# Query features of six tiles turned by VectorE and stored in blocks, and the last gate of pairs one pair sooner

## The chip, the cores and the metric

The kernel runs on one core of a Trainium2 chip. The metric is the device time of one execution in microseconds (us). Before the change the median of three runs is 624.48 us, from 624.06 to 625.14.

The engines are TensorE (PE in the profile; the loading of its weights is PEld), VectorE (DVE), ScalarE (ACT), GpSimd (POOL) and SyncE (SP). Transfers are issued from the queues of SP, ScalarE and GpSimd, each of which works in order, and move on the same 16 DMA engines.

## The reference

The input `x` has 2048 rows of 512. After a layer norm of each row, two branches are computed and added to `x`:

```python
# A: linear attention with 32 heads of 16
q, k, v = split(xn @ wqkv)
phi_q = concat(softmax(q w_phi), softmax(-q w_phi))    # per head: 32 features
phi_k = concat(softmax(k w_phi), softmax(-k w_phi))
kv  = sum_s phi_k v ;  z = sum_s phi_k
o   = (phi_q kv) / (phi_q z + 1e-6)
A   = o @ wo
# B: gated mlp that mixes over the sequence
z   = gelu(xn @ w_in) ;  z1, z2 = halves of z, 688 columns each
g   = w_sp @ layernorm(z2) + b_sp
B   = (z1 * g) @ w_out
out = x + A + B
```

## The kernel before

The 2048 rows are 16 tiles of 128 (`NT = 16`), and the tiles go in 8 pairs (`NP`). Most products are made in three parts of rounded values: a matrix is split into a rounded part and the rest of it, and `mm3` (lines 54 to 58) issues three matmuls. The rounding (L48) and the rest (L52) are helpers, so many operations carry these two lines and are told apart by their tiles.

The work comes in stages. In the first, all 16 tiles are projected; the unnormalised features of the queries, `e`, with the reciprocals of their softmax sums, go to `e_d` in DRAM. In the second and third, `z2` is made and multiplied by `w_sp` in a form with seven products (tile `g`, from about 228 to 488 us). As each pair of row tiles of that product is drained, `gate` (L783) multiplies it by `z1`, turns the result in blocks of 32x32 on VectorE (L796), and stores it with four DMAs, one for each 32 partitions (L799), in `u_d`. The DMAs put every block in its place, so `u_d` holds the whole transpose and can be loaded as it is for the product with `w_out`. The gate of the last pair, tiles 14 and 15, is put off into the last stage, where it is emitted after pair `GATE_LAST`.

The last stage runs from about 488 us to the end. It takes the pairs in order, and for the pair of tiles i and i+1 does the following:
- `project_u(i)` (L960) multiplies the gated rows `u` of tile i by `w_out` into a PSUM tile `pout`, 17 matmuls.
- `attend` (L943) multiplies the turned query features `f` of the pair by `kvT`, 16 products into `po` (32 instructions in the profile). The result is split into a rounded part by ScalarE and a rest by VectorE, tile `oT`.
- `project_u(i+1)` does the same for the other tile.
- `project_o` (L969) multiplies `oT` by `wo` into the same `pout`. ScalarE copies it to `xr` (L984), one of three buffers, and GpSimd's queue adds it to the output with an accumulating DMA (L985). The last tile goes another way, through VectorE and SP.
- `ahead` (L1008), after each tile, emits what later tiles need: `features(i+3)`, the load of `e` for tile i+5 (`et`), the load of `u` for tile i+4.
- `attend_T` (L926) makes the turned features of the next pair: 16 transposes on TensorE into `ptq` (L935 or L937), and four copies by ScalarE into the tiles `f` (L939), of which there are `NG + 1 = 5`, four to a pair.

`features` (L898) calls `q_fin` (L539): VectorE multiplies `e` by the sum of the key features `zb` into a temporary tile (L543, `qtmp`), sums it (L544), makes the reciprocals (L545 to L548) and multiplies `e` by them (L550). Then a DMA on GpSimd's queue copies the features to a tile `er` that TensorE can transpose in its faster type (L906).

The order of the instructions on each engine comes from a planner, which goes through the program in a simulated time and puts on each engine's queue what is ready. `tc.issue_after(x)` holds the instructions emitted inside it behind x, on x's own engine alone; it makes no engine wait for another. So the transposes of a pair stand behind the last product of the pair before on TensorE, and the features of each tile stand behind those of the tile before on VectorE. Semaphores are set by the data and the buffers.

Of the kernel before, what the change touches and what calls it, by code (L numbers as in the profile page):

```python
# [10 lines left out]
F32 = mybir.dt.float32  # L11
# [7 lines left out]
P = 128  # L19
# [4 lines left out]
NG = 4  # L24
NF = 2 * D
# [3 lines left out]
BL = 32  # L29
EPS_LN = 1e-5  # L30
EPS_DEN = 1e-6
XB = 5
FT, LT = 6, 13
NP = NT // 2
HP, QP = P // 2, P // 4
FP = 3 * P
# [4 lines left out]
def mixer(ctx: ExitStack, tc: tile.TileContext, x, x_t, wv, wqkT, phi_bd, wo, w_in, wst, b_r, w_out, out):  # L41
    nc = tc.nc
    pe, act, dve, pool, sp = nc.tensor, nc.scalar, nc.vector, nc.gpsimd, nc.sync
# [27 lines left out]
    def xz_tile(n, dt, name):  # L71
        return xz.tile([P, SL], dt, tag="xz", name=name)[:, :n]

    mid = ctx.enter_context(ExitStack())
    dram = ctx.enter_context(tc.tile_pool(name="dram", bufs=1, space=DRAM))
# [2 lines left out]
    u_d = dram.tile([NT, FU, P], F32, name="u_d")  # L78
    kvT_d = dram.tile([P, D], F32, name="kvT_d")
    zb_d = dram.tile([P, NF], F32, name="zb_d")  # L80
    nm_d = dram.tile([NT, ND, P], F32, name="nm_d")

    ident = cst.tile([P, P], F32, name="ident")
# [13 lines left out]
    def heads(ap):  # L97
        return ap.rearrange("p (h d) -> p h d", d=DH)

    def group(e, j):  # L100

        return e[:, j * P:(j + 1) * P]

    def pairs(ap, a):
        return ap.rearrange("p (h a) -> p h a", a=2)[:, :, a]

    def bc(ap, n):
        return ap.unsqueeze(2).to_broadcast([P, n, DH])
# [25 lines left out]
    def zproj(ps, s, w, order=(0, 1)):  # L134

        if ps in (za, kv_ps_p):
            p = [ps.tile([P, D], F32, tag="z", name="zps") for _ in range(2)]
        else:
            q = ps.tile([P, 2, D], F32, tag="z", name="zps")
            p = [q[:, k] for k in range(2)]  # L140
        t = xT[s]
        for k, j in enumerate(order):
            for c in range(ND):
                cs = slice(c * P, (c + 1) * P)
                zproj.last = mm3(p[k][:, :FC], (t[:, 0, cs], t[:, 1, cs]), (w[j][0][:, c], w[j][1][:, c]), c == 0, c == ND - 1)
        return [(slice(k, k + 1), p[k][:, :FC].unsqueeze(1)) for k in range(2)] if ps in (za, kv_ps_p) else [(slice(0, 2), q[:, :, :FC])]
# [28 lines left out]
    with ExitStack() as p0:  # L175
        res = p0.enter_context(left("p0res", 1))
        wk = p0.enter_context(left("p0wk", 2))
# [234 lines left out]
        t = xz_tile(2 * D, F32R, "xT").rearrange("p (a b) -> p a b", a=2)  # L412
# [18 lines left out]
        p = ps.tile([P, D], F32, tag="mm", name="proj")  # L431
# [7 lines left out]
        p = ps.tile([P, D], F32, tag="mm", name="proj")  # L439
# [18 lines left out]
        p = ps.tile([P, D], F32, tag="mm", name="proj")  # L458
# [80 lines left out]
    def q_fin(et, tmp, zb):  # L539

        e, r, t, w = et[:, :NF], *(et[:, NF + k * 2 * H:NF + (k + 1) * 2 * H] for k in range(3))
        den = et[:, NF + 6 * H:QW]
        dve.tensor_tensor(tmp, e, zb, op=ALU.mult)  # L543
        dve.tensor_reduce(t, heads(tmp), axis=AX.X, op=ALU.add)  # L544
        dve.tensor_tensor(t, t, r, op=ALU.mult)  # L545
        dve.scalar_tensor_tensor(den, pairs(t, 0), EPS_DEN, pairs(t, 1), op0=ALU.add, op1=ALU.add)
        dve.reciprocal(den, den)
        dve.tensor_tensor(w.rearrange("p (h a) -> p h a", a=2), r.rearrange("p (h a) -> p h a", a=2),  # L548
                          den.unsqueeze(2).to_broadcast([P, H, 2]), op=ALU.mult)
        return e, dve.tensor_tensor(heads(e), heads(e), bc(w, 2 * H), op=ALU.mult).ins  # L550

    QC = 4
    NQ = NT // QC
    NC = NP * NQ


    SEQ = [(i, q) for i in range(NP) for q in (range(NQ) if i < NP - 1 else (1, 2, 3, 0))]

# [5 lines left out]
    def load_a(n):  # L564
        i, q = SEQ[n]
        f = []
        for k in range(2):
            t = ws.tile([P, QC, P], F32, tag=f"f{k}", bufs=2, name="wf")
            sp.dma_start(t, wst[2 * i + k, :, q * QC:(q + 1) * QC, :])
            f.append(t.rearrange("p (k two) t -> p two k t", two=2))  # L570
        return f

    def prep_a(n, f):

        a, b = f
        pl = hl[n % 2]
        ops = {}

        def parts(names, src):
            t = pl.tile([P, 2, len(names), 2, P], F32R, tag="".join(names), name="A")  # L580
            prep_a.last = b_parts(t[:, 0], t[:, 1], src)
            for k, m in enumerate(names):
                ops[m] = t[:, 0, k], t[:, 1, k]

        sums = (sm[0].tile([P, 4, 2, P], F32, name="S") if sm else
                zw.tile([P, 4, FC], F32, tag=("T", "z2")[n], bufs=n + 1, name="S").rearrange("p a b -> p (a b)")[:, :8 * P].rearrange("p (a k b) -> p a k b", a=4, k=2))
        parts(("A11", "A12"), a)
        dve.tensor_tensor(sums[:, 0], b[:, 0], b[:, 1], op=ALU.add)
        dve.tensor_tensor(sums[:, 1], sums[:, 0], a[:, 0], op=ALU.subtract)  # L589
        parts(("S1", "S2"), sums[:, 0:2])  # L590
        dve.tensor_tensor(sums[:, 2], a[:, 0], b[:, 0], op=ALU.subtract)
        dve.tensor_tensor(sums[:, 3], a[:, 1], sums[:, 1], op=ALU.subtract)
        parts(("S3", "S4"), sums[:, 2:4])
        parts(("A22",), b[:, 1:2])
        return ops
# [3 lines left out]
    with ExitStack() as p1:  # L599
        tmp1 = p1.enter_context(left("tmp1", 1))  # L600
        kvT = tmp1.tile([P, D], F32, name="kvT")
        zb = tmp1.tile([P, NF], F32, name="zb")
# [41 lines left out]
        for s in range(NE):  # L644
            et = load_q(s, tb.tile([P, QW], F32, name="et") if s else tmp1.tile([P, 4, D], F32, tag="zhl", name="et").rearrange("p a b -> p (a b)")[:, :QW])
            tmp = zw.tile([P, 4, FC], F32, tag="z2", bufs=2, name="qtmp").rearrange("p a b -> p (a b)")[:, :NF]
            e, _ = q_fin(et, tmp, zb)
# [57 lines left out]
    for s in range(NT):  # L705
        p = zproj((kv_ps_p, zc, zbp, za)[s % 4], s, w2, (0, 1) if s % 2 == 0 else (1, 0))
# [7 lines left out]
        for k, q in p:  # L714
            ins = act.activation(z[:, k], q, AF.Gelu_apprx_tanh, scale=r_x[:, s:s + 1]).ins
# [35 lines left out]
    def load_z1(i):  # L751
        t = gt.tile([P, 2, FH + REM], F32, tag="z1", name="z1t")
        for k in range(2):
            pool.dma_start(t[:, k, :FH], z1_d[2 * i + k])  # L754
        return t

    def products(n, g):
        i, q = SEQ[n]
        ops = A.pop(n)
        for name, an, bn in FORM:  # L760
            if n % NQ == 0:
                g[name] = psg.tile([P, D], F32, tag="g", name="g")
            dst = g[name][:, :FC]
            for k in range(2):
                (ah, al), (bh, bl) = ops[an], B[2 * q + k][bn]
                mm3(dst, (ah[:, k], al[:, k]), (bh, bl), n % NQ == 0 and k == 0, n % NQ == NQ - 1 and k == 1)
# [16 lines left out]
    def gate(i, cb, z, u, ut, after=None):  # L783
# [10 lines left out]
        def turn():  # L794
# [3 lines left out]
            for b in range(0, P, BL):  # L798
                (pool if i == NP - 2 else sp).dma_start(dst[:, :, b:b + BL], src[b:b + BL].rearrange("p (m b) -> p m b", b=BL))  # L799

        return turn

    def slot(name, dt=F32):
        return xz_tile(2 * FH, dt, name)
# [44 lines left out]
    g, es, ets = {}, {}, {}  # L849
    for n in range(NC):  # L850
        i = SEQ[n][0]
        if n % NQ == 1 and i < NP - 1:
            z = load_z1(i)
        products(n, g)
        if n % NQ == NQ - 1 and i < NP - 1:
            c = gt.tile([P, 2, FU], F32, tag="c", name="c")
            cq = c[:, :, :FH].rearrange("p k (j f) -> p k j f", j=2)
            cb = drain(i, g, cq)
            g = {}
        if n + 3 < NC:  # L860
            raw[n + 3] = load_a(n + 3)
        if n + 2 < NC:
            A[n + 2] = prep_a(n + 2, raw.pop(n + 2))
        if n % NQ == NQ - 1 and i < NP - 1:
            turn = gate(i, cb, z, c, z, prep_a.last)
# [4 lines left out]
        if n == NC - 3:  # L870
            zs = slot("zb", F32R)
            zb, ident_r = zs[:, :NF].bitcast(F32), zs[:, NF:NF + P]
# [5 lines left out]
        if n == NC - 2:  # L878
            es[0], es[1] = first_q(0), first_q(1)
            t = xz_tile((KF + 1) * P, F32R, "u1")  # L880
# [10 lines left out]
    wk = ctx.enter_context(left("cwk", 2))  # L891
# [5 lines left out]

    def features(s):  # L898
        with tc.issue_after(fin[-1]):
            es[s], ins = q_fin(ets.pop(s), slot("qtmp")[:, :NF], zb)  # L900
        fin.append(ins)
        if s == 3:
            return
        e = es[s]
        es[s] = cw.tile([P, NF], F32R, tag="er", bufs=6, name="er")
        lasts[6] = pool.dma_start(es[s].bitcast(F32), e).ins  # L906
# [19 lines left out]
    def attend_T(s):  # L926

        fs = []
        for g in range(NG):
            pt = pst.tile([P, 2, 2, P], F32, tag="tr", name="ptq")  # L930
            for a in range(2):
                for k in range(2):
                    src = group(es[s + k], 2 * g + a)
                    if src.dtype == F32:
                        pe.transpose(pt[:, a, k], src, ident)  # L935
                    else:
                        pe.transpose(pt[:, a, k].bitcast(F32R), src, ident_r)  # L937
            f = wk.tile([P, 2, 2 * P], F32, tag="f", bufs=NG + 1, name="f")
            lasts[5] = act.activation(f, pt.rearrange("p a k b -> p a (k b)"), AF.Copy).ins  # L939
            fs.append(f)  # L940
        return fs
# [47 lines left out]
                dve.tensor_tensor(xr[:, cs], q, xr[:, cs], op=ALU.add)  # L989
                sp.dma_start(out[rows, cs], xr[:, cs])  # L990

    GATE_LAST = 8

    fT = attend_T(0)
    wk.tile([P, D], F32, tag="xr", bufs=3, name="xr")
# [21 lines left out]
    p, nxt = {}, dict(enumerate(uT))  # L1017
    for i in range(0, NT, 2):
# [17 lines left out]
        if i == 2:  # L1036
            with tc.issue_after(lasts[6]):
                z = load_z1(NP - 1)
        if i == GATE_LAST:
            with tc.issue_after(lasts[0]), tc.issue_after(lasts[1]):  # L1040
# [38 lines left out]
```

## Time and profile before

| | |
|---|---|
| median of three runs | 624.48 us (624.06 to 625.14) |
| the profiled execution, its own time | 623.2 us |
| its span in the profile | 621.5 us |
| granted clock of TensorE, mean | 0.999 |
| TensorE busy | 614.0 us, 99% of the span |
| VectorE busy | 507.9 us, 82% |
| ScalarE busy | 272.4 us, 44% |
| GpSimd busy | 114.0 us, 18% |
| DMA | 103.67 MB, mean 167 GB/s |

The profile shows one execution. Its span is the time between the first and the last recorded event; 1.7 us of the execution's own time lie around it. Busy time counts an engine's own instructions, not what it waits for. The chain that ended last is followed back from the last instruction, at each step to what released it, so its shares say which engine set the end. A row of instructions in order of time gives its start in us from the start of the span, its length, the engine, the line of the kernel, the operation, the tile written and the tiles read, and how many instructions were merged (x4); what stands in square brackets is the idle time of the engine before it and what ended it. Matmul ends are modelled, since matmuls overlap.

### The profile page before, as it was taken

How to read it: one execution, taken by the hardware profiler on the slowest of the kernel's cores; microseconds unless marked ns; L12 is line 12 of the kernel's file. 1: busy time of each engine (PE TensorE's matmuls, PEld its weight loads, DVE VectorE, ACT ScalarE, POOL GpSimd, SP SyncE). 2: the span in 40 equal slices, each digit the busy share in tenths (PEclk: the TensorE clock that was granted, in tenths of full speed). 3: DMA queues.
4: the chain of work that ended last, by engine and by line, in shares of the span. 5: the costliest groups of instructions: out<-in, count | busy, mean ns of one | idle time of the engine just before them, and what ended most of it. 6: DMA issues, size and time to landing. Idle time of an engine off the chain costs nothing.

```text
span 621.5 us, 11434 instructions
## 1 busy us (share of the span) xinstructions
PE 614.0 (99%) x4366; PEld 560.7 (90%) x4366; DVE 507.9 (82%) x903; ACT 272.4 (44%) x436; POOL 114.0 (18%) x198
## 2 busy tenths in 40 slices
PE   8999999999999999999999999999999999999997
PEld 6888888888889999999999999999999887778775
DVE  5999999999977598988979978696969899989211
ACT  5653334323523458885434433343344433334331
POOL 4122333232110025441000000000000212211110
PEclk9999999999999999999999999999999999999999
DMA  8557875665555857002464754637367799984732
GB/s 321 189 137 165 220 188 162 163 162 154 127 163 150 280 210 263 0 1 82 117 139 134 189 100 148 149 100 176 86 196 231 210 311 322 329 244 109 157 41 49
DMA packets 90671, 103.67 MB, mean 167 GB/s; under 512 B 47080, under 2 KB 60136, under 8 KB 90376
## 3 DMA queue, kind: packets, MB, share of 16 engines
q1 hardware_dynamic: 76840, 60.76, 33.9%
q0 software_dynamic: 11472, 36.54, 23.6%
q10 hardware_dynamic: 2304, 5.64, 2.3%
q8 instruction: 34, 0.56, 0.4%
q14 instruction: 21, 0.17, 0.1%
HBM read 61.61 MB, written 30.56 MB: 148 GB/s over the span
## 4 chain that ended last, share of the span: by engine, by line
PE 98%; DVE 1%; ACT 0%; POOL 0%; issue 0%; DVEq 0%; POOLq 0%
PE g L58 11%; PE g L57 11%; PE g L56 11%; PE proj L57 7%; PE proj L56 7%; PE proj L58 7%; PE zps L56 6%; PE zps L58 6%; PE zps L57 6%; PE pout L56 6%; PE pout L58 5%; PE pout L57 5%; PE ptq L937 1%; PE po L952 1%; PE kvps L353 1%; PE pout L966 1%
## 5 line engine op out<-in xcount | busy, mean ns | idle before, releaser
L57 PE MATMUL g<-B,A 128*128 128x344 f32 x448 | 143.3, 320 | 0.0
L56 PE MATMUL g<-B,A 128*128 128x344 f32 x448 | 142.8, 319 | 0.0
L58 PE MATMUL g<-B,A 128*128 128x344 f32 x448 | 140.6, 321 | 0.1
L56 PEld LDWEIGHTS g<-B,A 128*128 128x128 f32 x448 | 84.3, 188 | 0.0
L57 PEld LDWEIGHTS g<-B,A 128*128 128x128 f32 x448 | 84.2, 188 | 0.0
L58 PEld LDWEIGHTS g<-B,A 128*128 128x128 f32 x448 | 83.6, 188 | 0.4 <-DVE A L52 0.4
L48 ACT ACTIVATE A<-S 128x512 fp32r<-128x512 f32 x64 | 39.3, 629 | 76.9 <-DVE S L589 56.2
L56 PE MATMUL proj<-wqk_h,xT 128*128 128x512 f32 x128 | 50.1, 391 | 0.0
L58 PE MATMUL proj<-wqk_h,xT 128*128 128x512 f32 x128 | 49.8, 389 | 0.0
L57 PE MATMUL proj<-wqk_l,xT 128*128 128x512 f32 x128 | 49.8, 389 | 0.0
L121 ACT ACTIVATE e<-e,r_x 128x1024 f32<-128x1024 f32 x26 | 29.8, 1148 | 42.1 <-DVE e L120 41.1
L48 ACT ACTIVATE A<-wf 128x512 fp32r<-128x512 f32 (+1 forms) x64 | 33.1, 519 | 32.7 <-DMA wf<-in_wst 12.7
L52 DVE TENSOR_TENSOR A<-S,A 128x512 fp32r<-128x512 f32 x64 | 42.9, 686 | 5.4 <-ACT A L48 5.1
L56 PE MATMUL zps<-w_0h,xT 128*128 128x344 f32 x128 | 41.1, 321 | 0.0
L56 PE MATMUL zps<-w_1h,xT 128*128 128x344 f32 x128 | 40.9, 319 | 0.0
L58 PE MATMUL zps<-w_0h,xT 128*128 128x344 f32 x128 | 40.8, 319 | 0.0
L58 PE MATMUL zps<-w_1h,xT 128*128 128x344 f32 x128 | 40.6, 319 | 0.0
L57 PE MATMUL zps<-w_1l,xT 128*128 128x344 f32 x128 | 40.6, 317 | 0.0
L57 PE MATMUL zps<-w_0l,xT 128*128 128x344 f32 x128 | 40.6, 317 | 0.0
L754 POOL DMA_DIRECT2D z1t<-z_d x16 | 8.7, 546 | 167.0 <-DMA u_d<-z1t 101.1
L52 DVE TENSOR_TENSOR A<-wf,A 128x512 fp32r<-128x512 f32 (+1 forms) x64 | 35.0, 549 | 1.9 <-ACT A L48 1.8
L124 DVE TENSOR_REDUCE sm<-e 128x64 f32<-128x1024 f32 x26 | 31.1, 1199 | 2.5 <-ACT e L121 2.4
(218 smaller groups left out, 1425.7 us busy)
## 6 DMA issues: line engine op xcount, KB each, us to landing
wf<-in_wst SPq DMA_DIRECT2D x64, 256.0 KB, 3.3
e_d<-e POOLq DMA_DIRECT2D x16, 544.0 KB, 5.0
et<-e_d SPq DMA_DIRECT2D x16, 544.0 KB, 5.8
er<-et POOLq DMA_DIRECT2D x12, 512.0 KB, 5.9
z_d<-z1f ACTq DMA_DIRECT2D x16, 344.0 KB, 3.0
z1t<-z_d POOLq DMA_DIRECT2D x16, 344.0 KB, 5.0
zacc<-e POOLq DMA_DIRECT2D x10, 512.0 KB, 4.9
u<-u_d SPq DMA_DIRECT2D x15, 320.0 KB, 6.1
```

Source lines behind the costliest of these rows:

```text
L48: return act.activation(h, src, AF.Copy).ins
L52: return (eng or dve).tensor_tensor(l, src, h.bitcast(F32), op=ALU.subtract).ins
L56: pe.matmul(dst, ah, bh, start=start, stop=False)
L57: pe.matmul(dst, ah, bl, start=False, stop=False)
L58: return pe.matmul(dst, al, bh, start=False, stop=stop).ins
L121: softmax_pair.last = less, act.activation(e, e, AF.Exp, scale=scale).ins
L124: dve.tensor_reduce(sm, heads(e), axis=AX.X, op=ALU.add)
L353: i = pe.matmul(kv_acc[k:k + QP, m // 4], vs[:, m * QP:(m + 1) * QP], e[:, m * HP:(m + 1) * HP], start=first and m < 4 and len(ready) == n ...
L754: pool.dma_start(t[:, k, :FH], z1_d[2 * i + k])
L937: pe.transpose(pt[:, a, k].bitcast(F32R), src, ident_r)
L952: lasts[3] = pe.matmul(po[r][c * QP:(c + 1) * QP, k], kvT[rows, m // 2, cols], fs[m // 4][rows, m // 2 % 2], start=True, stop=True).ins
L966: lasts[2] = pe.matmul(p, rt, w, start=False, stop=i == NT - 1 and k == 1).ins
```

## The change

`TQ = 10` is new. For tiles 10 to 15, `features` no longer copies the features to `er`. It turns them in 32x32 blocks on VectorE, back into the temporary tile, and stores that in a new DRAM tensor `q_d` with four DMAs on GpSimd's queue, one for each 32 partitions, as `gate` does for its rows. `attend_T` for the pairs 10/11, 12/13 and 14/15 then has no transposes and no copies: it emits four DMAs on SP's queue that load the tiles `f` from `q_d`, 256 KB each. They stand in the same `issue_after` block as the transposes did, but that block names an instruction of TensorE and so doesn't hold them.

`GATE_LAST` is 6 in place of 8: the gate of tiles 14 and 15 is emitted after the pair 6/7, with its four stores on SP's queue.

```diff
+TQ = 10
...
+    q_d = dram.tile([NP, NF, 2, P], F32, name="q_d")
...
+    def turn_q(s, dst, e, eng=sp):
+
+        ins = dve.transpose(dst, e).ins
+        q = q_d[s // 2, :, s % 2].rearrange("(m j) t -> j m t", j=BL)
+        for b in range(0, P, BL):
+            turn_q.last = eng.dma_start(q[:, :, b:b + BL], dst[b:b + BL].rearrange("p (m t) -> p m t", t=BL)).ins
+        return ins
+
+    def load_f(s, f, g):
+        sp.dma_start(f, q_d[s // 2, 2 * g * P:2 * (g + 1) * P].rearrange("(a p) k t -> p a (k t)", p=P))
+        return f
...
     def features(s):
         with tc.issue_after(fin[-1]):
-            es[s], ins = q_fin(ets.pop(s), slot("qtmp")[:, :NF], zb)
+            tmp = slot("qtmp")[:, :NF]
+            es[s], ins = q_fin(ets.pop(s), tmp, zb)
+            if s >= TQ:
+                ins = turn_q(s, tmp, es.pop(s), pool)
         fin.append(ins)
+        if s >= TQ:
+            return
...
     def attend_T(s):
 
         fs = []
+        if s >= TQ:
+            return [load_f(s, wk.tile([P, 2, 2 * P], F32, tag="f", bufs=NG + 1, name="f"), g) for g in range(NG)]
...
-    GATE_LAST = 8
+    GATE_LAST = 6
```

## The prediction

> **What bounds the kernel now.** I read first the page's busy shares and its chain that ended last, to see which engine sets the end:
>
> ```profile
> span 621.5 us, 11434 instructions
> PE 614.0 (99%) x4366; PEld 560.7 (90%) x4366; DVE 507.9 (82%) x903; ACT 272.4 (44%) x436; POOL 114.0 (18%) x198
> PE 98%; DVE 1%; ACT 0%; POOL 0%; issue 0%; DVEq 0%; POOLq 0%
> ```
>
> TensorE is on the chain for 98% of the span. So an instruction taken off TensorE is worth its own length, as long as nothing that replaces it arrives late; work added elsewhere costs nothing until TensorE waits for it. Next, the busy times in steps of 16 us, about one pair of tiles each in the last stage (columns: stretch, its length, busy us and count of PE, PEld, DVE, ACT, POOL, granted clock, share of the DMA engines, GB/s):
>
> ```profile
> 537.00:553.00 16.00, 16.00 (x109) 12.73 (x107) 15.24 (x25) 5.72 (x10) 2.88 (x5) 1.00 0.92 293
> 553.00:569.00 16.00, 16.00 (x110) 12.73 (x108) 13.97 (x23) 6.97 (x11) 3.56 (x5) 1.00 0.44 117
> 569.00:585.00 16.00, 16.00 (x110) 12.75 (x108) 8.44 (x12) 5.73 (x11) 2.92 (x5) 1.00 0.75 151
> 585.00:601.00 16.00, 16.00 (x110) 12.73 (x109) 2.94 (x4) 5.83 (x11) 1.84 (x3) 1.00 0.36 76
> ```
>
> TensorE is busy all 16.00 us of each row. VectorE is nearly full until 569 and mostly free after; GpSimd uses at most 3.56 of 16; the DMA engines have room from 553 on. Last, the chain in order of time around the three pairs that the change touches (start, length, what): the transposes of the query features (ptq), the start of the next tile's `pout`, and the products that read the features (po):
>
> ```profile
> 558.38 1.02 PE po L952 x32
> ...
> 568.99 1.34 PE ptq L937 x16
> 570.33 0.30 PE pout L56
> 570.63 0.23 PE pout L57
> ...
> 574.30 1.02 PE po L952 x32
> ...
> 584.91 1.31 PE ptq L937 x16
> ...
> 590.20 1.02 PE po L952 x32
> ...
> 600.81 1.34 PE ptq L937 x16
> ...
> 606.11 1.02 PE po L952 x32
> ```
>
> These are pairs 10/11, 12/13 and 14/15. Their 48 transposes stand on the chain; nothing else runs on TensorE meanwhile.
>
> **What goes from TensorE.** 1.34 + 1.31 + 1.34 = **3.99 us**. The 12 copies from PSUM into `f` go from ScalarE too; it is at most 6.97 of 16 busy, so that is worth nothing.
>
> **What VectorE gets.** Six block transposes of 128x1024. The nearest row is the gate's own, of 1472 columns:
>
> ```profile
> 489.58 1.70 DVE L796 STREAM_TRANSPOSE z1t<-c 128x1472 f32<-128x1472 f32 x1
> 491.21 0.78 DVE L52 TENSOR_TENSOR ul<-u,uh 128x640 fp32r<-128x640 f32 x1
> 491.94 2.62 DVE L52 TENSOR_TENSOR wol<-wof,woh 128x512 fp32r<-128x512 f32 x4
> ...
> 546.79 1.22 DVE L550 TENSOR_TENSOR et<-et 128x1024 f32<-128x1024 f32 x1
> ...
> 558.50 0.83 DVE L52 TENSOR_TENSOR ul<-u,uh 128x640 fp32r<-128x640 f32 x1 [1.83 <-ACT uh L48]
> 559.24 0.22 DVE L548 TENSOR_TENSOR et<-et 128x64 f32<-128x64 f32 x1
> 559.49 1.22 DVE L550 TENSOR_TENSOR et<-et 128x1024 f32<-128x1024 f32 x1
> 560.64 1.22 DVE L543 TENSOR_TENSOR qtmp<-et,zb 128x1024 f32<-128x1024 f32 x1
> 561.77 1.28 DVE L52 TENSOR_TENSOR oT<-po,oT 128x512 fp32r<-128x512 f32 x2
> ...
> 565.19 1.58 DVE L789 TENSOR_TENSOR z1t<-z1t,c 128x1376 f32<-128x1376 f32 x1
> ...
> 569.65 1.71 DVE L796 STREAM_TRANSPOSE zt<-z1t 128x1472 f32<-128x1472 f32 x1
> ...
> 575.15 1.22 DVE L550 TENSOR_TENSOR et<-et 128x1024 f32<-128x1024 f32 x1
> ```
>
> By columns, 1.70 x 1024/1472 = 1.18 us each, 7.1 in all. The three L550 rows shown end the features of tiles 11, 13 and 15: 548.0, 560.7 and 576.4. The last gate moves with its two large instructions (1.58 and 1.71, 3.3 us; its small ones add some tenths) one pair, 16 us, sooner, so from 565 to about 549. After 576.4 VectorE has little to do, and the delay dies there.
>
> **What the queues get.** GpSimd loses six copies of features (er) and gets 24 stores; SP gets 12 loads of `f`, 256 KB each, and issues the gate's four stores sooner. The rows (start, length, engine; SPq is SP's queue), then the page's sizes and median times from issue to landing:
>
> ```profile
> 491.91 3.64 POOL L799 DMA_DIRECT2D u_d<-z1t  x4 [36.52 <-ACT woh L48]
> ...
> 553.30 1.79 POOL L985 DMA_DIRECT2D out<-xr  x2 [4.21 <-issue]
> ...
> 576.92 0.54 POOL L906 DMA_DIRECT2D er<-et  x1 [6.06 <-DVE et L550]
> ```
>
> ```profile
> 550.38 0.55 SPq L536 DMA_DIRECT2D et<-e_d  x1
> 571.39 5.95 SPq L799 DMA_DIRECT2D u_d<-zt  x4
> 583.11 0.38 SPq L814 DMA_DIRECT2D u<-u_d  x1
> ```
>
> ```profile
> wf<-in_wst SPq DMA_DIRECT2D x64, 256.0 KB, 3.3
> ...
> u<-u_d SPq DMA_DIRECT2D x15, 320.0 KB, 6.1
> ```
>
> The gate's four block stores are the same form as a tile's new ones (32 partitions, runs of 32 floats), 46 blocks a row against 32. On GpSimd they took 3.64 us to issue, 0.91 each, against 0.54 for an er copy. So two tiles cost GpSimd 7.3 us a pair where it had 1.1: with 3.56 busy, 9.8 of 16. That fits. Behind a store that waits for its transpose stand the accumulations into the output. Tile 6's was issued at 553.30; its buffer of `xr`, one of three, is written again for tile 9, whose last product ends at 568.99. Those 15.7 us cover 1.18 + 3.64 of new delay. The path from a block store on SP to a readable result is bounded above by 583.11 - 571.39 = 11.7 us, since the load of `u` behind it reads what it stored. I take 11.7 as the slow end, with 3.64, the issue alone, as the fast end. A load of `f` I take between 3.3 (same size, quiet) and 6.1, with about 1.2 us for issuing the three ahead of the last (0.38 each, the u row).
>
> **Are they in time?** A load needs both tiles' stores. Only the first of its four buffers is spare: there are five, so the other three loads wait for the po of the pair before.
> - Pair 10. Tile 11 is turned at 548.0 + 2 x 1.18 = 550.4, or 553.7 with the gate's 3.3 ahead of it. Slow end: 553.7 + 11.7 + 6.1 + 1.2 = 572.7. Fast end: buffers free after the po before (a pair earlier, 559.4), so 559.4 + 3.3 + 1.2 = 563.9. Wanted: 574.30 - 1.34 = 572.96.
> - Pair 12. Tile 13 is turned at 560.7 + 4 x 1.18 + 3.3 - 1.83 (the idle time at 558.50 absorbs that much) = 566.9. Slow end: 566.9 + 19.0 = 585.9. Wanted: 590.20 - 2.65 = 587.5.
> - Pair 14. Tile 15: 576.4 + 7.1 - 1.83 = 581.7 (the gate was ahead of it before too). Slow end 600.7. Wanted: 606.11 - 3.99 = 602.1.
>
> So even the slow ends just make it: 0.3, 1.6 and 1.4 us to spare. I cost the new work at nothing. The cover is those 16 us between one pair's po and the next; if it goes, each microsecond late at po costs one, but only once, since the chain that makes features hardly waits for TensorE (1.83 us at 558.50) and a delayed pair moves the later deadlines too. The moved gate costs nothing either way: its result feeds only the loads of `u` for tiles 14 and 15, issued at 583.11 for pair 14 at 601. SP is empty between 550.38 and 571.39, so the earlier stores meet no queue; a load of `f` behind them waits at most for their 5.95 us of issue, which lies within the 11.7. If the loads of `u` stand behind those of pair 12 in turn, they go after 566.9 + 11.7 = 578.6, still ahead of 583.11.
>
> The row at 491.91 bears on one more cost: three of its four issues ran beside VectorE's four subtractions (491.94 to 494.56), and all took 0.91 each, so no hold shows there. The Trainium skill, "SBUF — State Buffer", section "SBUF: two separate sides", speaks against the choice of queue: GpSimd writes the descriptors of its own transfers through a port that it shares with VectorE, and some VectorE instructions keep it locked out until they end. By that rule the time would be that of the third rival below.
>
> **The sum.** 621.5 - 3.99 = 617.5 of span; the profiled execution took 623.2 with 1.7 around it, so 619.2. That execution was 1.3 under the median 624.48, against which the runs are told: 624.48 - 3.99 = 620.5. Small waits at the new seams I estimate at 0.2: **620.7**.
>
> **Rivals.**
> 1. *Pair 10 comes late.* SP works in order, and the loads of `u` for tiles 14 and 15 wait for the gate's stores. Before, the first of these was issued 571.39 - 565.19 = 6.2 us after the gate's product started, and read 11.7 later; with the product at 549, the loads of `u` go at 566.9. If the loads of `f` stand behind them, they go some 2 us later (four issues of about half a microsecond, an estimate from the 0.38), at 568.9, and the last is there at 568.9 + 1.2 + 3.3 to 6.1 = 573.4 to 576.2: 0.4 to 3.2 late, 620.9 to 623.7, 622.3 in the middle. For: SP's order is the planner's, and both kinds become ready near 560. Against: the loads of `f` come first in the program, and the pairs after have no such load ahead.
> 2. *VectorE's order hurts.* The rests of the attention output (oT) must be done before `project_o`. At 561.77 + 1.28 they end at 563.05, and this row shows when they are needed:
>
> ```profile
> 563.04 0.47 PE pout L966 x2
> ```
>
> That is 563.51, 0.46 us to spare. A transpose (1.18) or the gate's product (1.58) queued in front makes TensorE wait 0.7 to 1.1 us, in each of the pairs 6, 8 and 10: 2.1 to 3.3 of the 3.99 are gone, 622.6 to 623.8. Against: L543 already stood in front there, so a further instruction must be added to it, not put in its place.
> 3. *Slower: GpSimd's issues are held up by VectorE.* If each of a tile's four stores waits out one VectorE instruction of 1.22 to 1.71 us, the stores are done 4.9 to 6.8 us later, and pair 10 is late by that less 0.3 if all else is at its slow end. Paid once, less 3.99: +0.6 to +2.5, so 625.1 to 627.0, slower by over 0.2% from a hold of 5.5 us a tile on (0.3 + 3.99 + 1.25). Against: the row at 491.91. For: the issues of er (shortest, median and longest in ns), of which one took 942 against 545:
>
> ```profile
> L906 POOL DMA_DIRECT2D er<-et x6: 527/545/942, 541.8 to 576.9; - x6
> ```
>
> [...]
>
> That the transposes stay is no rival: the branch for these tiles has none.
>
> **How the numbers follow.** Chances: forecast 0.58, pair 10 late 0.17, VectorE's order 0.15, held issues 0.10. A measurement of this kernel can tell about 0.2%, 1.25 us, from no change. Faster, under 623.2: 0.58, most of 0.17 and half of 0.15, some 0.80, of which I keep 0.78, as two of the cases can fall together. Within 0.2%: the rest of these two and the mild end of the third, 0.13. Slower: 0.09. The likeliest alone lies between 620.0 and 621.5. The range runs from 619.6 (all 3.99, the seam behind each transpose that shows 0.30 in place of the 0.23 of a `pout` inside, and a spread of 0.66 between runs, as 625.14 stands over 624.48) to 623.7, which takes in the first rival and most of the second and leaves the third out.
>
> **What would show it.** Right: no ptq on TensorE after 555; the pairs of the last 48 us at 14.6 in place of 15.9; po starting right behind pout; six transposes of about 1.18; store issues of about 0.9 on GpSimd. Wrong: idle time of TensorE ended by a load of `f` at po (first and third rival: then look whether store issues are above 0.94) or by VectorE's oT ahead of `project_o` (second).

## The result and the profile after

The change made the kernel slower: 633.46 us in the median of six runs (631.88 to 634.95) against 624.9 for the kernel before beside it, a ratio of 1.0141 with a 95% interval from 1.0125 to 1.0158. The profiled execution took 633.56 us. The line numbers are up to 21 higher than before (L813 are the gate's stores, L828 and L829 the loads of `u`, L559 the new stores, L563 the loads of `f`, L973 is po, L987 the end of `project_u`).

The page of the changed kernel, the lines that answer to those shown of before:

```profile
span 631.8 us, 11362 instructions
PE 613.6 (97%) x4318; PEld 558.1 (88%) x4318; DVE 515.9 (82%) x909; ACT 268.4 (42%) x424; POOL 129.9 (21%) x216
...
PE 93%; DMA 3%; DVE 2%; issue 1%; POOL 1%; ACT 0%; DVEq 0%; POOLq 0%
```

The 48 transposes are gone (4366 to 4318 matmuls), but DMA, which was not on the chain at all, now is. The waits of TensorE from 480 us on (line, who was waited for, us in total, times, longest):

```profile
PE po L973 <- DMA f<-q_d: 11.0, 1, 11.0
PE ptq L958 <- DVE c L786: 0.2, 1, 0.2
```

One wait, for the loads of `f`. The chain in order of time shows where, and what came behind it:

```profile
558.64 1.02 PE po L973 x32
...
577.54 6.47 DMA f<-q_d
584.01 0.14 issue
584.15 3.16 PE po L973 x32
587.30 0.72 PE pout L57
...
592.07 0.47 PE pout L987 x2
...
601.89 1.02 PE po L973 x32
...
606.54 0.47 PE pout L987 x2
```

Pair 10 waits until 584.15; pairs 12 and 14 don't wait. But po of pair 10 then takes 3.16 in place of 1.02, and the `project_u` behind it 592.54 - 587.30 = 5.24 in place of the 607.01 - 602.91 = 4.10 behind pair 12. Two things lengthen po. Its products read four tiles `f`, and the first wait covers only the first of them; the weight loads for the other three waited too (who waited for `f`, us, times):

```profile
PEld po L973: 1.5, 3
```

The clock is the second (columns as in the table of 16 us stretches; the clock is the third number from the end):

```profile
575.00:577.00 2.00, 0.00 (x0) 0.00 (x0) 1.28 (x2) 0.00 (x0) 0.00 (x0) 0.75 1.10 234
577.00:579.00 2.00, 0.00 (x0) 0.00 (x0) 0.00 (x0) 0.00 (x0) 0.00 (x0) 0.50 1.06 241
...
587.00:589.00 2.00, 2.00 (x8) 1.48 (x5) 1.02 (x2) 1.09 (x2) 0.00 (x0) 0.50 0.79 244
589.00:591.00 2.00, 2.00 (x9) 1.54 (x9) 2.00 (x3) 0.00 (x0) 0.28 (x1) 0.83 0.30 106
```

The wait began at 584.15 - 11.0 = 573.1. The granted clock fell to 0.50 some three microseconds into it and came back some five after its end. At half the clock the 1.02 of po would be 2.04 (an estimate), so at most 1.02 of the 2.14 more is the clock's, and the rest is waiting for the later tiles `f`. The account closes: 11.0 of waiting, 2.14 more in po, 1.14 more in `project_u` at the low clock, less 3.99 of transposes, is 10.3; the spans differ by 631.8 - 621.5 = 10.3. The medians differ by less, 8.6.

What held up the loads is seen on SP's queue, in order of time:

```profile
556.66 9.72 SPq L813 DMA_DIRECT2D u_d<-zt  x4
566.42 2.36 SPq L538 DMA_DIRECT2D et<-e_d  x1
574.38 0.38 SPq L828 DMA_DIRECT2D u<-u_d  x1
574.86 2.47 SPq L829 DMA_DIRECT2D rt<-u_d  x2
577.54 3.11 SPq L563 DMA_DIRECT2D f<-q_d  x4
```

The gate's stores came 15 us sooner, but took 9.72 us to issue (5.95 before); the first load of `u` could go only 574.38 - 556.66 = 17.7 us after the first store (11.7 before); and the loads of `f` stood behind it. The stretches of 16 us show what those transfers met:

```profile
537.00:553.00 16.00, 16.00 (x108) 12.71 (x108) 15.33 (x24) 6.96 (x11) 5.58 (x8) 1.00 0.95 231
553.00:569.00 16.00, 16.00 (x108) 12.74 (x107) 14.93 (x21) 5.73 (x10) 8.27 (x11) 1.00 0.96 150
569.00:585.00 16.00, 4.96 (x31) 3.48 (x33) 6.82 (x10) 1.33 (x2) 4.60 (x6) 0.72 1.05 239
```

Before the change the DMA share of these was 0.92, 0.44 and 0.75. Now all three are full, the middle one at 150 GB/s. (A share can come out above 1, so these shares are rough.)

### The profile page after: what moved, and what is told of

Same layout as the page of the kernel before. It is cut to its first block, busy times and chain, and to the rows that moved or that the text cites. A ratio compares the mean times of both kernels' runs of the same rounds, so it can differ in the third digit from the quotient of the medians.

```text
span 631.8 us, 11362 instructions
## 1 busy us (share of the span) xinstructions
PE 613.6 (97%) x4318; PEld 558.1 (88%) x4318; DVE 515.9 (82%) x909; ACT 268.4 (42%) x424; POOL 129.9 (21%) x216
## 4 chain that ended last, share of the span: by engine, by line
PE 93%; DMA 3%; DVE 2%; issue 1%; POOL 1%; ACT 0%; DVEq 0%; POOLq 0%
PE g L59 10%; PE g L58 10%; PE g L57 10%; PE proj L58 7%; PE proj L57 7%; PE proj L59 7%; PE zps L59 6%; PE zps L57 6%; PE zps L58 6%; PE pout L57 5%; PE pout L59 5%; PE pout L58 5%; PE po L973 2%; PE kvps L355 1%; DMA out<-xr 1%; PE pout L987 1%
```

## The experiments

Theory A (A' later on) said that the place of the loads of `f` on SP did it; theory B (called D later on) that the DMA engines had no time; theory C that the moved gate disturbs VectorE's order by itself. Times are medians; a ratio is worked out from the runs and not from two medians, so it can differ a little from theirs.

**1. The gate alone moved.** `TQ = 10` becomes `TQ = NT`, so no tile is turned by VectorE.

> Only the gate is moved; all tiles keep their transposes on TensorE. Theory A (order on SP: the loads of f for pair 10 stand behind loads of u that wait for the gate's stores) and theory B (DMA time: the 128-byte runs of the new stores fill the DMA engines, so everything lands late) both expect the time of before, 624.9 within 1.2, since no f is loaded. Theory C (the moved gate disturbs VectorE's order by itself) expects 627 or more.

624.43, ratio 0.9998 (0.9981 to 1.0014): no difference, so theory C falls. But its stretches show what the move does to the DMA engines:

```profile
553.00:569.00 16.00, 16.00 (x108) 12.74 (x107) 13.09 (x21) 5.83 (x11) 3.10 (x6) 1.00 0.95 210
569.00:585.00 16.00, 16.00 (x109) 12.71 (x108) 7.43 (x11) 5.81 (x11) 2.90 (x5) 1.00 0.50 123
```

The gate's stores and the loads behind them fill by themselves the stretch that was 0.44 busy.

**2. The turning alone.**

```diff
-    GATE_LAST = 6
+    GATE_LAST = 8
```

> Gate left where it was before; six tiles are turned by VectorE. The loads of f for pair 10 then stand ahead of the gate's stores on SP, and those for pair 12 ahead of the loads of u. A expects no wait of TensorE at po and the 3.99 us of transposes gained: 620.5 to 621.5. B expects a wait of 2 us or more at pair 10 or 12 all the same, since 24 stores of 128-byte runs remain: 623 to 630.

633.71, ratio 1.0149 (1.0133 to 1.0164), as slow as the whole change. Its wait and its SP queue:

```profile
PE po L973 <- DMA f<-q_d: 10.5, 1, 10.5
```

```profile
564.43 3.46 SPq L563 DMA_DIRECT2D f<-q_d  x4
574.28 11.62 SPq L813 DMA_DIRECT2D u_d<-zt  x4
586.26 10.32 SPq L563 DMA_DIRECT2D f<-q_d  x4
```

Pair 10 is in time now; pair 12 waits 10.5 us instead, since the gate's stores, now at 574, meet those of tiles 13 to 15 and take 11.62 us to issue. The loss moved to where the gate is. A's forecast is out by 12 us. B is right that a wait stays, but its range ended at 630.

**3. Loads of `f` ahead of loads of `u`.** The changed kernel, and on SP:

```diff
...
-        if i + 4 < NT:
+        if i + 4 < TQ + 4:
             us[i + 4] = fetch_u(i + 4)
+        elif i + 4 < NT:
+            with tc.issue_after(load_f.last):
+                us[i + 4] = fetch_u(i + 4)
```

> As the changed kernel, but on SP the loads of u for tiles 14 and 15 are queued behind the four loads of f for pair 10. A expects the loads of f to go when SP is through with the gate's stores and the load of et behind them, near 569 in place of 577.5, so that the wait of 11.0 us falls to about 2.5 and the clock stays up: 622 to 624. B expects most of the wait to stay, as the stores themselves land late: 628 or more.

631.89, ratio 1.0112 (1.0093 to 1.0131). The loads went when A said, yet TensorE waited 9.5 us in place of 11.0:

```profile
PE po L973 <- DMA f<-q_d: 9.5, 2, 8.3
```

```profile
557.03 9.53 SPq L813 DMA_DIRECT2D u_d<-zt  x4
566.60 2.61 SPq L538 DMA_DIRECT2D et<-e_d  x1
569.46 5.80 SPq L563 DMA_DIRECT2D f<-q_d  x4
```

Eight microseconds of place on the queue were worth 1.5 of waiting: the transfers themselves were slow. The four loads took 5.80 us to issue in place of 3.11, and up to 10.8 from issue to landing in place of 6.5. B's forecast holds.

**4. Loads of `u` first, the new stores in whole rows.** The order on SP is the changed kernel's but for one load of `u`. The blocks are not put in their places:

```diff
-            turn_q.last = eng.dma_start(q[:, :, b:b + BL], dst[b:b + BL].rearrange("p (m t) -> p m t", t=BL)).ins
+            turn_q.last = eng.dma_start(q_d[s // 2].rearrange("c k t -> (c k t)")[s % 2 * NF * P:(s % 2 + 1) * NF * P].rearrange("(p n) -> p n", n=NF)[b:b + BL], dst[b:b + BL]).ins
...
-        if i + 4 < NT:
+        if i + 4 < TQ + 4:
             us[i + 4] = fetch_u(i + 4)
...
+        if i + 2 == TQ:
+            us[14], us[15] = fetch_u(14), fetch_u(15)
...
```

> As the changed kernel, with the loads of u for tiles 14 and 15 written ahead of the loads of f for pair 10 (the order on SP that the changed kernel has but for one load), and the new stores writing each partition's 4 KB as one run, so that the turned blocks aren't put in their places in q_d and the attention of tiles 10 to 15 is wrong. A alone (the gate's stores are slow of themselves) expects the wait at pair 10 to stay near 11: 631 to 634. B (the new stores' 128-byte runs hold up the gate's stores, and so the loads behind them) expects the gate's stores to land in some 12 us as before the change, the loads of f to go near 571 and a wait of 1 to 3: 621 to 625.

630.1, ratio 1.0096 (1.0066 to 1.0127): between the two, whose ranges ended at 625 and began at 631. The gate's first store to the first load of `u` fell from 17.7 to 566.60 - 556.47 = 10.1 us, as B said, and the loads of `f` went from 568.37 on; but TensorE still waited 5.6 us, and the clock fell. So even with the new stores in whole rows, the place behind the gate and the loads of `u` is enough to be late.

**5. Both: loads of `f` first, the new stores in whole rows.** The edits of 3 and the first of 4.

> As the run with the loads of f ahead of those of u, but the new stores write each partition's 4 KB as one run (the blocks aren't put in their places in q_d, so the attention of tiles 10 to 15 is wrong). Theory D (the runs of 32 floats fill the DMA engines until the pair's time) expects that with both the order and the runs changed the loads of f for pair 10 land before 573 and TensorE waits under 1 us there: 620 to 621.5. Theory A' (what holds up f is the place behind the gate's four stores on SP, whatever the runs) expects the wait of 8 us to stay within 2: 629 to 632.

620.11, ratio 0.993 (0.9903 to 0.9956), and no wait for `f` at all; the one wait left that counts is for VectorE:

```profile
PE pout L59 <- DVE oT L53: 0.8, 1, 0.8
```

This is the whole gain: 624.24 - 620.11 = 4.1 us, against 3.99 of transposes. A' falls, D holds. Against run 3, with the same bytes and the same rule for the order, it differs in the length of the runs that the new stores write. The page's line on GpSimd's transfers, first of run 3, then of run 5 (packets, MB, share of 16 engines over the span):

```profile
q0 software_dynamic: 11760, 36.54, 25.6%
```

```profile
q0 software_dynamic: 11760, 36.54, 24.2%
```

25.6% of 630.0 is 161.3 us, 24.2% of 618.4 is 149.7: the six tiles' stores cost 11.6 us more in blocks, 1.9 a tile. That is no fixed price: in run 12 below, with the same new stores in blocks but shorter transfers of the gate beside them, the line shows 25.2% of 620.2 = 156.3, which is 1.1 a tile. The planner also put one load of `f` ahead of the gate's stores here and two ahead of the load of `et`, so the order isn't the same to the last instruction; run 12 has the order of run 3.

**6. TensorE kept at work through the wait.** 48 matmuls without use ahead of the products of pair 10:

```diff
+        if i == TQ:
+            with tc.issue_after(lasts[2]):
+                idle = pst.tile([P, D], F32, tag="tr", name="idle")
+                for k in range(48):
+                    lasts[2] = pe.matmul(idle, wo_h[:, k % ND, :P], wo_h[:, 0], start=True, stop=True, skip_group_check=True).ins
```

> As the changed kernel, with 48 matmuls without use, 0.23 us each and 11 us in all, put on TensorE in front of the products of pair 10, so that TensorE works while it would wait. If the slow stretch behind the wait (granted clock 0.50 until about 590) is a consequence of the idle time, the clock stays at 1.00 and some 3 us come back: 630 to 631.5. If the clock falls for another reason, or if the wait is the whole loss, the time stays at 633 to 634.

636.12, ratio 1.0186 (1.0154 to 1.0217): above both of the expected ranges. The stretches show that the clock did stay up while TensorE worked, and fell after the short waits that were left (2.2 us in three pieces, the longest 1.2):

```profile
577.00:581.00 4.00, 4.00 (x19) 3.34 (x18) 3.65 (x7) 0.00 (x0) 3.11 (x4) 1.00 1.08 279
581.00:585.00 4.00, 2.78 (x16) 2.00 (x19) 2.52 (x3) 0.00 (x0) 1.11 (x2) 1.00 1.06 298
585.00:589.00 4.00, 3.06 (x33) 0.75 (x33) 0.00 (x0) 0.05 (x1) 1.99 (x3) 0.80 1.07 299
```

and within the last of them:

```profile
588.00:589.00 1.00, 1.00 (x11) 0.19 (x5) 0.00 (x0) 0.05 (x1) 0.00 (x0) 0.50 0.91 227
```

But the loads of `f` ended later here: the last part of po began at 587.13. In this run VectorE went on with tiles 14 and 15 (GpSimd busy 3.11 in the first row; no store there in the changed kernel), and their stores shared the engines with the loads. So here the low clock followed the idle time, but its price could not be had back this way, and the time above the changed kernel's isn't accounted for.

**7. From tile 12 on.** `TQ = 12`, the gate as changed.

> The changed kernel with VectorE's turning from tile 12 on, so that pair 10 keeps its transposes on TensorE; the gate stays one pair sooner. D expects the stores of tiles 12 to 15 to follow the gate's stores instead of meeting them, f for both pairs in time, and two of three gains, 2.65 us: 621 to 622. A' expects the loads of f, which stand behind the gate's stores and the loads of u here too, to be in time as well, since those are over by 568. If VectorE's order or GpSimd's issues were the cause, pair 12 would wait as pair 10 did: 626 or more.

622.2, ratio 0.9951 (0.9933 to 0.9969): faster than before, near what D said, but from 619.68 to 629.86 in 13 runs. The profiled execution, 628.41, is one of the long ones:

```profile
PE po L973 <- DMA f<-q_d: 5.3, 2, 3.1
```

So the loads of pair 12 come about when they are wanted, and are late in some executions: the mean granted clock is 0.993 in this one and 0.992 in the other long one (629.86), 0.999 or 1.0 in the eleven shorter ones.

**8. From tile 12 on, the gate as before.** `TQ = 12`, `GATE_LAST = 8`.

> As the run from tile 12 on, with the gate where it was before the change. Its stores then meet those of tiles 13 to 15 from 572 on. D expects f for pair 12 late by 5 us or more, as in the run with the gate left in place and six tiles (10.5), since the same transfers share the engines there: 627 to 632. If only the total of the new traffic mattered, two tiles fewer would bring most of the loss back: 622 to 624.

625.87, ratio 1.0023 (0.9995 to 1.005): no measurable difference. D expected 627 to 632 and was wrong on what would be late: `f` was in time, and the loads of `u` behind it were not. ScalarE stood still for `u` of tile 14 with the copies of `oT` queued behind it, and TensorE waited 3.1 us for `oT`:

```profile
585.15 0.60 ACT L1005 ACTIVATE xr<-pout 128x512 f32<-128x512 f32 x1 [1.04 <-PE pout L59]
596.03 0.74 ACT L49 ACTIVATE uh<-u 128x640 fp32r<-128x640 f32 x1 [10.28 <-DMA u<-u_d]
596.67 1.07 ACT L49 ACTIVATE oT<-po 128x512 fp32r<-128x512 f32 x2
```

**9. From tile 12 on, the gate two pairs sooner.** `TQ = 12`, `GATE_LAST = 4`: two pairs sooner than before the change.

> VectorE turns tiles 12 to 15, and the last gate runs two pairs sooner than before the change, so its stores are issued near 540 and are over before the new stores begin at 557. If what makes pair 12 late is that these stores share the DMA engines (theory D), f is in time in every execution, 2.65 us are gained, and the spread of the run from tile 12 on with the gate at its changed place (619.7 to 629.9) closes: 621 to 622.5. If the stores of tiles 12 to 15 alone are too much, the waits and the spread stay: 622 to 628.

621.31 (620.28 to 622.75), ratio 0.9943 (0.9921 to 0.9966): faster than both kernels, and in four runs without the spread of run 7. No wait for `f` is left, but one of 1.0 us for VectorE's `oT`:

```profile
PE pout L59 <- DVE oT L53: 1.0, 1, 1.0
```

**10. From tile 10 on, the gate two pairs sooner.** `TQ = 10`, `GATE_LAST = 4`.

> The changed kernel with the last gate yet one pair sooner, emitted after the pair 4/5. On SP the loads of f for pair 10 then have no store of the gate and only one load of u behind them. D expects the gate's 5 us of DMA time to fall into a stretch that is full already (share 1.04 from 521), pushing the rest back; the loads of f for pair 10 wait for stores alone: 621 to 626, with less than half of the changed kernel's wait. A' (the place on SP behind the gate) expects the whole gain: 620.5.

628.59, ratio 1.0065 (1.0045 to 1.0085). Both expected less. The profiled execution took 1328.25 us, twice the others, and was long from its first stage on, so its trace tells nothing of them. Their mean granted clock, 0.992 to 0.995, is near that of executions with long waits, so TensorE probably waited here too; for what stays open, and neither theory accounts for it.

**11. Tiles 14 and 15 alone.** `TQ = 14`, `GATE_LAST = 6`.

> VectorE turns only tiles 14 and 15; the gate stays where the change put it. Two tiles' stores fall after 571, when the gate's are over. D expects no wait and one pair's gain, 1.33 us: 623, with a spread like that of the kernel before. If any new store made TensorE wait, 625 or more.

622.83, ratio 0.9986 (0.9955 to 1.0017). TensorE shows no wait in the last stage, as D said, but one pair's 1.33 us isn't told from no change.

**12. Loads of `f` first, the gate's stores in whole rows.** The edit of run 3, the new stores in blocks, and in `gate`, for the last pair, a store of `src[b:b + BL]` as whole rows, whose blocks are then not in their places.

> As the run with the loads of f ahead of those of u, with the new stores in blocks as in the changed kernel, but the last gate's four stores write each partition's row as one run (the blocks of tiles 14 and 15 aren't put in their places in u_d, so the product with w_out of these two tiles is wrong). The order on SP is the same as in that run. If it is the sum of DMA time that counts (D), some 3 us less of it for the gate lets the loads of f go some 3 to 6 us sooner, near 564 to 566, and TensorE's wait at pair 10 falls from 9.5 to between 1 and 6, paid at least in part by the clock: 622 to 629. If the runs of the gate's stores alone were the cause, no wait is left: 620 to 621. If the runs of the new stores alone were, nothing changes: 631 to 632.

622.71, ratio 0.9992 (0.9967 to 1.0017), against 631.89 for run 3. TensorE's wait fell from 9.5 to 2.1 us (0.69 at pair 10, 1.40 at pair 12) in the profiled execution, which took 621.89; four of the ten took 625.0 to 626.9:

```profile
PE po L976 <- DMA f<-q_d: 2.1, 2, 1.4
```

```profile
556.32 5.49 SPq L814 DMA_DIRECT2D u_d<-zt  x4
...
564.43 3.24 SPq L563 DMA_DIRECT2D f<-q_d  x4
```

D's forecast holds (622 to 629, a wait of 1 to 6, the loads of `f` near 564 to 566). With the loads of `f` first, shortening either the gate's transfers or the new ones brings pair 10 nearly or wholly into time, so what counts there is the sum of the two. The place on SP counts beside it, as runs 3 and 4 show: neither the order nor the rows alone is enough.

The five runs with the gate at its changed place and six tiles turned, side by side:

| order on SP | new stores | gate's stores | wait for f, us | time, us |
|---|---|---|---|---|
| u first | blocks | blocks | 11.0 | 633.46 |
| f first | blocks | blocks | 9.5 | 631.89 |
| u first | rows | blocks | 5.6 | 630.1 |
| f first | blocks | rows | 2.1 | 622.71 |
| f first | rows | blocks | none | 620.11 |

## Why the prediction was wrong

It forecast 620.7, faster, and gave 0.09 to slower. By its steps:

**What goes from TensorE: right.** 3.99 us were there to be had: run 5 got 4.1.

**What VectorE and GpSimd get: right.** The transposes took 1.24 us each (1.18 predicted), the store issues 0.83 in the median and 1.14 at most (0.91). The third rival needed 1.22 or more in each of them, so it fell. The rule of the Trainium skill that it drew on ("SBUF — State Buffer", "SBUF: two separate sides") speaks of VectorE instructions in a mode that uses two ports, not of all; no run here shows whether one of these was in that mode, so the rule is neither borne out nor refuted.

**"Slow ends": the step that failed.** The prediction took 11.7 us, from the gate's first store to the first load behind it, as the upper bound of the path of a store, and 6.1 as that of a load. That was the time of those transfers in a stretch with room. In the changed kernel the same path took 17.7 us, and the loads of `f`, once issued, up to 6.5 (10.8 in run 3). With the gate moved and no tile turned (run 1) the path took 564.74 - 552.90 = 11.8 us, so the bound held there, and the 6 us more came with the new stores. A time read from one trace is no bound when the change adds to what it shares.

The DMA time was never summed. The page's lines on the two queues that the change touches, of the changed kernel and then of the kernel before, would have been the price:

```profile
q1 hardware_dynamic: 80104, 63.91, 35.1%
q0 software_dynamic: 11760, 36.54, 25.4%
```

```profile
q1 hardware_dynamic: 76840, 60.76, 33.9%
q0 software_dynamic: 11472, 36.54, 23.6%
```

GpSimd's transfers took 160.5 us of all engines' time in place of 146.7, SP's 221.8 in place of 210.7: 13.8 for six tiles' stores (less the er copies that they replace), 11.1 for the three pairs' loads. Until pair 10 was wanted, four of the six tiles and one of the three pairs had to go: 9.2 + 3.7 = 12.9. The moved gate brings (0.95 - 0.44) x 16 = 8.2 more by run 1. That is 21 us, and the rows quoted in the prediction had 1.3 + 9.0 = 10.3 free from 537 to 569. The difference, 10.8, is near the 11.0 waited, by chance in part, since neither stretches nor shares are that sharp. The same reckoning for run 5 gives 2.0 for four tiles' stores, 2.7 for a pair's loads and 8.2, together 12.9 against 10.3, and run 5 shows no wait; so it is out by some microseconds. Nor does a full share tell of lateness by itself: run 5 has 0.96 from 553 to 569 as the changed kernel has, but moves 201 GB/s there in place of 150. Still the sum could be had roughly beforehand, from the gate's four stores and the loads in the trace, and would have shown that there was no room to spare.

"The DMA engines have room from 553 on" and "the moved gate costs nothing either way" were each true of one move alone. Run 1 shows the second; it also shows that the moved gate uses up the room that the first speaks of.

**The first rival** named the place (the loads of `f` behind those of `u`), but gave 0.4 to 3.2 us for it, from the same 11.7, where 11.0 were measured. By its sum the loads of `u` would go at 566.9 and those of `f` at 568.9; they went at 574.38 and 577.54, and the first of the four landed 6.47 later. Run 3 shows that the place alone explains 1.5 of the 11.0 while the engines are full.

**"Each microsecond late at po costs one, but only once"** was right as to "once" (pairs 12 and 14 didn't wait), and wrong in two of its grounds. The low clock added up to 1.02 + 1.14 = 2.2 us to the waiting. The Trainium skill ("TensorE: Matmul & The Clock Gate", "What's actually happening") says that the clock halves after at least one window of about 3.4 us without work and returns after at least one such window of work; the trace agrees roughly as to the fall, some 3 us after 573.1, and gives some five for the return. And the chain of features does wait for TensorE: VectorE works in order, and stood 11.67 us behind `oT` of pair 10, with the turning of tile 14 and the features of tile 15 queued after it (row of the changed kernel's VectorE):

```profile
587.98 1.29 DVE L53 TENSOR_TENSOR oT<-po,oT 128x512 fp32r<-128x512 f32 x2 [11.67 <-ACT oT L49]
```

**The second rival** is there at its size but not its count: one wait of 0.8 us for `oT` in run 5, one of 1.0 in run 9.

**The forecast's own signs.** Three of its signs of being right (no ptq after 555, transposes and issues as sized) came true beside a result on the other side. The one that po starts right behind `pout` failed at pair 10, and the sign of being wrong, idle time of TensorE ended by a load of `f` at po, came true; only these two told.

## What to carry to other kernels

Where a change moves work from the engine that bounds to the DMA engines, add up their time stretch by stretch, new transfers and moved ones together, against the free share of each stretch, up to the moment when the first result is wanted; the time that a transfer takes in a trace with room is no bound for it. The sum is rough, to some microseconds here, but it tells whether there is room to spare. A move that costs nothing by itself (the gate, run 1) can use up the room that another counts on; and leaving it where it was is no cure when its transfers only meet the new ones elsewhere (run 2). A wait of some microseconds on TensorE can cost its clock as well.

## What the runs showed of the hardware

The same 4 KB of each partition cost the DMA engines 1.9 us a tile more as 32 runs of 128 bytes than as one (run 3 against run 5), and 1.1 more where the gate's transfers beside them were shorter (run 12 against run 5). The Trainium skill ("DMA: Bandwidth & Descriptors", "Specifications") puts the least transfer for full rate at 512 bytes, and the stretch from 553 to 569 agrees: 0.96 busy at 150 GB/s in the changed kernel, 0.96 at 201 in run 5 with the new stores in whole rows. Before the change the stretch from 537, which has no store in such runs, was 0.92 busy at 293. SP's issue was slower in the fuller stretch: four stores of the same form took 5.95 us to issue before the change, 8.20 in run 1 and 9.72 in the changed kernel, and 5.49 as whole rows (run 12). And even short waits can cost the clock: 2.2 us in three pieces were followed by a stretch at 0.50 (run 6), while single waits of 0.69 and 1.40 us, a pair apart, were not (run 12, 1.00 in both stretches).
